# A linear-attention and mixture-of-experts kernel: state increment in column halves, loads behind K, an exponential in place, and spaced-out negations

## The chip, the cores and the metric

The kernel runs on one core of a Trainium2 chip. The metric is the device time of one execution in microseconds (us); of several executions the median is taken. Everything is float32 in memory; TensorE works on float32 (two passes, and so two load and two multiply records, per multiply) and on float32 rounded to its own short form, named fp32r (one pass).

## The reference

Two stages follow each other: a gated linear attention with a complex decay, and a mixture of four experts with two matrices each.

```python
mag = np.sqrt(a_re * a_re + a_im * a_im)
scale = np.minimum(mag, 0.999) / (mag + 1e-06)
a_re_n, a_im_n = (a_re * scale, a_im * scale)
for t in range(S):                      # S = 768, B = 4, H = 8, D = 48
    new_re = ar * S_re - ai * S_im
    new_im = ar * S_im + ai * S_re
    kv = np.einsum('bhd,bhe->bhde', k[:, :, t], v[:, :, t])
    S_re, S_im = (new_re + kv, new_im)
    y[:, :, t] = np.einsum('bhd,bhde->bhe', q[:, :, t], S_re)
# x: y as (3072, 384); E = 4 experts, F = 1024
p = domain_probs / (domain_probs.sum(-1, keepdims=True) + 1e-09)
for e in range(E):
    h = np.maximum(x @ w1[e], 0.0)
    out += p[:, e:e + 1] * (h @ w2[e])
```

## The kernel before, in words

The 3072 rows are cut into 12 groups (g) of 256 rows, each of two chunks (c) of 128. In the first part of the program, up to some 597 us, TensorE computes the first two experts of group g-1 (`moe1`: `w1_step` writes `ph`, `w2_step` writes `po`) while the other engines prepare the attention of group g. In the second part (`fast_path` from the pool `fin` on) it computes the other two experts with a scheme of fewer products, whose order is written out by hand in the table `UNIT`.

Attention of one group: `norm` scales the decay A to a magnitude below 1 (squares, a logarithm, an exponential, one correction step, on ScalarE and VectorE). `prefix` forms the running products of A along the rows on VectorE. `finish` makes Q = q times A and K = k over A. Both are put into a layout by head: for groups 0 and 1 with TensorE, later by a trip through device memory (`trip`: Q to `q_d` to `Qst`, K to `k_d` to `Kst`), whose transfers the queue of SyncE (SP) issues. Then come, for each chunk, functions of `chunk`: `turned` turns K with TensorE (`ktp`) and ScalarE copies it to `KT` (112 columns a head: the real part in columns 0 to 47, zeros, the imaginary part from column 64 on); `scores` multiplies `Kst` and `Qst` (`sc`); `values` makes the output (`yp`, by pairs of heads whose results stand in partitions 0 to 63 and from 64 on), and `increment` adds K times v to the state (`dp`, 8 multiplies a chunk, 20 chunks: the last chunk of each of the 4 sequences needs none). `turn_x` and `store_y` pass y on.

What stands in which order: the first part is ordered by a scheduler that lists the instructions of each engine by its own estimate of times; `stream`, `advance` and `between` say in what order work is handed to it, and `behind` ties one instruction behind another. Loads of the next group's q, k and a (`load_qk`, `load_a`) are tied behind the last transfer of the group before (`last["q"]`), that is the return of K in most groups. In the second part `UNIT` is read row by row by `unit`: M is a multiply, C a copy, D a sum, H and L the hidden layer, F a piece of the second matrix, and ("B", n) does up to n pieces from the list `side`: preparing the next x (`prep_x`), and for the second matrix of the next half expert the negated copy (`rest` in `second_w`: ScalarE writes `slo` from `shi`, and then GpSimd's queue adds the weights to it by a transfer). A piece "gap" in `side` makes it wait for so many B rows.

In `norm` the two buffers `s` and `u` hold four values: m2 and L in `s`, y0 and v in `u`. The exponential (L396) reads L and writes y0, so it is the first to write `u`, whose space was that of Q of a group before, which the trip to `q_d` reads.

Of the kernel before, what the change touches and what calls it, by code (L numbers as in the profile page):

```python
# [8 lines left out]
F32 = mybir.dt.float32  # L9
F32R = mybir.dt.float32r  # L10
AF = mybir.ActivationFunctionType
# [4 lines left out]
B, H, S, D = 4, 8, 768, 48  # L16
HD = H * D
NT = B * S
E, F = 4, 1024
# [14 lines left out]
M = 112  # L34
IM = 64
# [21 lines left out]
NSEL = 2  # L57
# [64 lines left out]
def fast_path(ctx, tc, qkP, aP, vP, probsP, w, out, flag):  # L122
    nc = tc.nc
# [25 lines left out]
    for c in range(CG):  # L149
# [8 lines left out]

    late_d = {(e, h): dram.tile([P, 2, len(WORDER) * P], F32, name=f"late_d{e}_{h}")
              for e, h in ((E1, 0), (E1 + 1, 0), (E1 + 1, 1))}  # L160

    wts = {}
    whi = {}
# [127 lines left out]
    with ExitStack() as c1:  # L291
# [82 lines left out]
        last = {}  # L374

        def norm(g, A, parts=((0, SEG),), prev=(None, None)):
            s = tmp(f"s{g}")
            u = tmp(f"u{g}")
            for n, (lo, hi) in enumerate(parts):
                col = g if n == 0 else NG  # L380
                fs = slice(lo * MS, hi * MS)
                Af = A.rearrange("p c i m -> p c (i m)")[:, :, fs]
                m2, L, y0, v = s[:, 0, fs], s[:, 1, fs], u[:, 0, fs], u[:, 1, fs]
                ins = [nc.scalar.activation(m2, Af[:, 0], AF.Square)]
                sq = nc.scalar.activation(L, Af[:, 1], AF.Square)
                ins.append(nc.vector.tensor_tensor_reduce(m2, m2, L, scale=1.0, scalar=3e38,
                                                          op0=ALU.add, op1=ALU.min, accum_out=st_m2[:, col:col + 1]))
                for x, p in zip(ins + [sq], prev + prev[:1]):
                    if p is not None:
                        behind(x, p)  # L390
                if n > 0:
                    behind(ins[0], exp)
                    behind(sq, exp)
                yield 1.0
                ln = nc.scalar.activation(L, m2, AF.Ln, bias=m2b)
                exp = nc.scalar.activation(y0, L, AF.Exp, scale=-0.5, bias=lnb)  # L396
                if g == 1:
                    behind(ln, state["kt", 0, 1])
                    behind(exp, state["kst", 0, 1])
                if g == 0 and n == 0:  # L400
                    nc.vector.tensor_tensor(v, m2, y0, op=ALU.mult)
                    nc.vector.scalar_tensor_tensor(v, v, 4.0 / CAP ** 2, y0, op0=ALU.mult, op1=ALU.mult)
                else:
                    last["sq"] = nc.scalar.activation(v, y0, AF.Square, scale=2.0 / CAP)
                    nc.vector.tensor_tensor(v, m2, v, op=ALU.mult)
                last["lin"] = nc.scalar.activation(L, y0, AF.Identity, scale=2.0 * EPS / CAP, bias=neg1)
                yield 0.95
                nc.vector.scalar_tensor_tensor(y0, v, 3.0, y0, op0=ALU.subtract, op1=ALU.mult)
                yield 0.95
                nc.scalar.activation(v, v, AF.Square, bias=neg1, accum_out=st_w[:, col:col + 1])  # L410
                nc.vector.scalar_tensor_tensor(y0, y0, -1.0, L, op0=ALU.max, op1=ALU.mult)
                yield 0.95
                nc.vector.tensor_tensor(Af, Af, bc2(y0), op=ALU.mult)
                yield 1.75
# [132 lines left out]
        def chunk(g, c, K, y):  # L547
# [27 lines left out]
            def increment():  # L575
                if last:
                    return
                d_ps = ps_a.tile([M, H, D], F32, tag="pa", name=f"dp{g}_{c}")
                for h in range(H):
                    ins = nc.tensor.matmul(d_ps[:, h, :], KT[:, h, :], vc[:, h * D:(h + 1) * D], start=True, stop=True)  # L580
                    if g == 0 and c == 1:
                        behind(ins, wts["w1"])
                state["dp", g, c] = ins
                Gt = small.tile([M, H, D], F32, tag="G", name=f"G{g}_{c}")
                if first:
                    nc.scalar.activation(Gt, d_ps, AF.Copy, scale=-1.0)
                else:
                    nc.vector.tensor_tensor(Gt, state[g, c], d_ps, op=ALU.subtract)
                state[g, c + 1] = Gt
# [275 lines left out]

        def stream():
            for g in range(1, NG):
                qk = load_qk(g, last["q"])
                if g + 1 < NG:
                    A.append(load_a(g + 1, prev=last["q"]))  # L870
                for r in front(g, A[g], qk):
                    yield g, r
                if g + 1 < NG:
                    for r in norm(g + 1, A[g + 1]):
                        yield g, r
# [53 lines left out]
    with ExitStack() as c2:  # L929
# [289 lines left out]
        def unit(R, h, fill):  # L1219
            e = E1 + R // NB2  # L1220
            assert ("w", e, h) in ready
            W = quads[e, h]

            def at(x):
                return bank(x) if isinstance(x, int) else snap[f"C{h}" if x == "C" else x]

            k = 0
            for op in UNIT:
                if op[0] == "M":
                    _, r, b, start = op  # L1230
                    n = XOF[r]
                    assert ("x", R, n) in ready
                    prod(bank(b), W[r], X[n], start)
                    if h == 1 and last_use[n] == r:
                        freed.add(n)
                elif op[0] == "C":
                    act(at(op[1]), at(op[2]), scale=op[3] if len(op) > 3 else 1.0)
                elif op[0] == "D":
                    tt(at(op[1]), at(op[2]), at(op[4]), ALU.add if op[3] == "+" else ALU.subtract)
                elif op[0] in "HL":  # L1240
                    (hi_h if op[0] == "H" else lo_h)((R, op[2], 4 * h + op[1]), at(op[3]))
                elif op[0] == "F":
                    fill(k)
                    k += 1
                else:
                    bg(op[1])

        half = C2 * HD
# [11 lines left out]
        for R in range(NR2):  # L1260
            for h in range(2):
# [5 lines left out]
                if h == 0:  # L1267
                    side += todo_x[:1]
                    tail = []
                    if R == 0:  # L1270
                        side += todo_x[1:2] + [["gap", None, 4, None]] + late
                    elif R in (1, NB2):
                        casts, tail = fetch_w(E1 + 1, *((0, 10) if R == 1 else (1, 0)))
                        side += todo_x[1:2] + [["gap", None, 3, None]] + casts
                    else:
                        side += todo_x[1:2]
# [212 lines left out]
```

## Time and profile before

| | |
|---|---|
| median of 3 runs | 975.66 us (974.34 to 976.28) |
| the profiled execution's own time | 973.79 us |
| its span, first to last instruction | 972.0 us |
| matmuls (PE) busy, share of the span | 946.8 us, 97% |
| VectorE (DVE) busy | 739.2 us, 76% |
| ScalarE (ACT) busy | 478.2 us, 49% |
| granted TensorE clock, mean | 0.997 |

The profiled execution took 1.8 us more than its span, and 1.87 us less than the median of the runs. In the rows below, PE is TensorE's multiply, PEld its load of the stationary operand, and an entry like `[0.98 <-DVE pb L959]` says how long the engine was idle ahead of the row and what ended it. The ends of multiplies are modelled, so the argument goes by the starts of rows that follow each other. TensorE is busy nearly throughout from 50 us on; before that it waits for loads, norms and turned data.

### The profile page before, as it was taken

The numbers are of one execution on the slowest core, as the hardware profiler recorded it, in microseconds if no ns is written. First come the engines' busy times: TensorE is split into PE (matmuls) and PEld (weight loads), VectorE is DVE, ScalarE is ACT, GpSimd is POOL, SyncE is SP. The second block draws the span as 40 slices with busy tenths as digits, with TensorE's granted clock in tenths as the row PEclk, the third lists the DMA queues.
The fourth block names the chain that finished last, engine by engine and source line by source line (L and its number), as shares of the span: only waits on it lengthen the run. The fifth ranks groups of instructions, "written<-read, shape, count | busy, mean of one in ns | idle before, by whom it ended". The sixth has DMA issues, their size and how long they took to land.

```text
span 972.0 us, 17615 instructions
## 1 busy us (share of the span) xinstructions
PE 946.8 (97%) x6717; PEld 923.0 (95%) x6717; DVE 739.2 (76%) x1610; ACT 478.2 (49%) x952; POOL 165.7 (17%) x206
## 2 busy tenths in 40 slices
PE   5899999999999999999999999999999999999997
PEld 3799999999999999999999999899999999999997
DVE  7889989898998889878897375767584857576642
ACT  7756436355363735446254355545453545445430
POOL 6020000000000000000000025433433352322000
PEclk9999999999999999999999999999999999999999
DMA  9586276684856647484669399232514443131112
GB/s 299 188 157 161 66 188 145 158 167 141 181 135 152 169 124 178 133 220 112 167 159 346 146 275 271 61 100 66 144 44 134 161 113 106 50 98 50 50 50 77
DMA packets 112238, 139.56 MB, mean 144 GB/s; under 512 B 8016, under 2 KB 95872, under 8 KB 112144
## 3 DMA queue, kind: packets, MB, share of 16 engines
q1 hardware_dynamic: 100656, 111.42, 40.0%
q0 software_dynamic: 11488, 26.93, 11.8%
q8 instruction: 55, 0.90, 0.4%
q14 instruction: 39, 0.32, 0.1%
HBM read 89.82 MB, written 48.49 MB: 142 GB/s over the span
## 4 chain that ended last, share of the span: by engine, by line
PE 86%; DMA 4%; ACT 3%; DVE 3%; issue 1%; SPq 0%; DVEq 0%; ACTq 0%
PE pob L953 20%; PE ph L235 18%; PE po L256 17%; PE pb L953 17%; PE sc L595 4%; PE dp L580 2%; PE yp L617 2%; PE yp L612 2%; DMA Kst<-k_d 1%; PE ktp L562 1%; PE xp L647 1%; DMA k_d<-K 1%; DMA y_d<-y 1%; DMA xa<-y_d 1%; PE qp L452 0%
## 5 line engine op out<-in xcount | busy, mean ns | idle before, releaser
L953 PE MATMUL pob<-shi,hid 128*128 128x384 f32 x528 | 148.7, 335 | 0.5 <-DVE hid L962 0.5
L256 PE MATMUL po<-whi,hh 128*128 128x384 f32 x384 | 129.9, 339 | 0.9 <-ACT acc L725 0.9
L256 PE MATMUL po<-wlo,hh 128*128 128x384 f32 x384 | 128.9, 336 | 0.0
L245 ACT ACTIVATE hh<-ph 128x512 fp32r<-128x512 f32 x96 | 57.0, 594 | 114.9 <-PE ph L235 114.1
L965 POOL TENSOR_TENSOR Z<-Z 128x384 f32<-128x384 f32 x84 | 90.7, 1115 | 109.3 <-DVE xl L959 46.4
L235 PE MATMUL ph<-xha,whi 128*128 128x256 f32 x576 | 103.8, 287 | 1.2 <-ACT xha L222 1.2
L235 PE MATMUL ph<-xha,wlo 128*128 128x256 f32 x576 | 101.3, 283 | 0.0
L235 PE MATMUL ph<-xla,whi 128*128 128x256 f32 x576 | 100.7, 284 | 0.0
L953 PE MATMUL pb<-xh,shi 128*128 128x384 f32 x291 | 97.3, 336 | 1.0 <-DVE pb L959 1.0
L953 PEld LDWEIGHTS pob<-shi,hid 128*128 128x128 f32 x528 | 96.5, 188 | 1.2 <-DVE hid L962 1.1
L953 PE MATMUL pb<-xl,shi 128*128 128x384 f32 x288 | 96.4, 335 | 0.0
L953 PE MATMUL pb<-xh,slo 128*128 128x384 f32 x288 | 96.3, 335 | 0.0
L246 DVE SCALAR_TENSOR_TENSOR hl<-ph,hh 128x512 fp32r<-128x512 f32 x96 | 66.0, 687 | 34.8 <-ACT hh L245 34.1
L235 PEld LDWEIGHTS ph<-xha,whi 128*128 128x128 f32 x576 | 85.7, 190 | 2.9 <-ACT xha L222 1.7
L953 PE MATMUL pob<-slo,hid 128*128 128x384 f32 x264 | 88.3, 335 | 0.0
L256 PE MATMUL po<-whi,hl 128*128 128x384 f32 x384 | 84.9, 338 | 0.0
L235 PEld LDWEIGHTS ph<-xha,wlo 128*128 128x128 f32 x576 | 82.9, 191 | 0.0
L235 PEld LDWEIGHTS ph<-xla,whi 128*128 128x128 f32 x576 | 82.6, 191 | 0.2 <-issue 0.2
L956 ACT ACTIVATE SN<-pb 128x384 f32<-128x384 f32 x96 | 47.3, 492 | 67.1 <-PE pb L953 59.7
L959 DVE TENSOR_TENSOR xl<-Z,xh 128x384 fp32r<-128x384 f32 x104 | 59.9, 607 | 21.6 <-ACT xh L956 13.8
L256 PEld LDWEIGHTS po<-whi,hh 128*128 128x128 f32 x384 | 72.5, 189 | 1.5 <-ACT acc L725 1.3
L956 ACT ACTIVATE hid<-pb 128x384 fp32r<-128x384 f32 x76 | 37.2, 490 | 72.2 <-PE pb L953 71.8
(227 smaller groups left out, 2090.6 us busy)
## 6 DMA issues: line engine op xcount, KB each, us to landing
qk<-qkP SPq DMA_DIRECT2D x24, 384.0 KB, 7.2
acc_d<-acc POOLq DMA_DIRECT2D x24, 384.0 KB, 5.2
ACC<-acc_d SPq DMA_DIRECT2D x48, 192.0 KB, 3.0
A<-aP SPq DMA_DIRECT2D x22, 384.0 KB, 8.2
Z<-y_d SPq DMA_DIRECT2D x16, 384.0 KB, 4.5
q_d<-Q SPq DMA_DIRECT2D x12, 387.0 KB, 4.1
Qst<-q_d SPq DMA_DIRECT2D x12, 387.0 KB, 5.5
v<-vP SPq DMA_DIRECT2D x24, 192.0 KB, 2.4
```

Source lines behind the costliest of these rows:

```text
L235: ins = nc.tensor.matmul(ph[:, u, :], wt[:, j * P:(j + 1) * P], xt[:, j, :], start=(n == 0), stop=(n == 3 * NJ - 1))
L245: wts["hh"] = nc.scalar.activation(hh, ph, AF.Relu)
L246: nc.vector.scalar_tensor_tensor(hl, ph, 0.0, hh, op0=ALU.max, op1=ALU.subtract)
L256: ins = nc.tensor.matmul(po[t], part[0][:, u, t * P:(t + 1) * P], wts[i][n][:, HD:], start=(i % FE == 0 and part[0] is hh and n == 0), sto ...
L580: ins = nc.tensor.matmul(d_ps[:, h, :], KT[:, h, :], vc[:, h * D:(h + 1) * D], start=True, stop=True)
L595: ins = nc.tensor.matmul(s_ps[:, h, :], Kc[:, hf * 4 + h, :], Qc[:, hf * 4 + h, :], start=True, stop=True)
L612: ins = nc.tensor.matmul(yo, st[:, o:o + n], Qc[:, o // D, :], start=True, stop=False)
L617: ins = nc.tensor.matmul(yo, vc[:, o:o + n], sc[h // 4][:, h % 4, :], start=first, stop=True)
L953: return tc.keep_in_program_order(nc.tensor.matmul(*args, **kw))
L956: return pin(nc.scalar.activation(dst, src, fn, scale=scale))
L959: pin(nc.vector.tensor_tensor(dst, x, y, op=op))
L965: nc.gpsimd.tensor_tensor(dst, x, y, op=op)
```

## The change

There are four edits.

1. **State increment by column halves.** Each of the 8 multiplies of `increment` becomes two: columns 0 to 63 of `KT` into partitions 0 to 63, and columns 64 to 111 into partitions 64 to 111. v, the moving operand (48 columns), is streamed for each.
2. **Next loads behind K.** From group 3 on, a transfer of one element from `Kst` to device memory (`here_d`) is issued on SP ahead of the loads of q, k and a. It reads `Kst`, so SP's queue stands until K has landed.
3. **Exponential in place.** In `norm` m2 and y0 share `s`, v and L share `u`; the exponential reads and writes the same place, and the first to write `u` is the square behind it (L404 before).
4. **Late negations one by one.** In the first unit of the second part the four negations of a half expert stand apart by gaps of one, and one ("B", 2) row is read four rows later in the unit (R, h) = (0, 1), and only there.

```diff
-    ("F",), ("D", 1, 0, "+", "B"), ("H", 1, 1, "F"), ("B", 2),
+    ("F",), ("D", 1, 0, "+", "B"), ("H", 1, 1, "F"), ("B", 2, 0),
     ("M", 15, 4, False), ("H", 3, 0, 4),
-    ("M", 18, 2, False), ("L", 1, 1, "F"), ("L", 3, 0, 4), ("D", 3, 2, "+", "E"),
+    ("M", 18, 2, False), ("L", 1, 1, "F"), ("L", 3, 0, 4), ("D", 3, 2, "+", "E"), ("B", 2, 1),
...
+    here_d = dram.tile([1, 1], F32, name="here_d")
...
-                m2, L, y0, v = s[:, 0, fs], s[:, 1, fs], u[:, 0, fs], u[:, 1, fs]
+                m2, y0, v, L = s[:, 0, fs], s[:, 1, fs], u[:, 0, fs], u[:, 1, fs]
                 ins = [nc.scalar.activation(m2, Af[:, 0], AF.Square)]
-                sq = nc.scalar.activation(L, Af[:, 1], AF.Square)
-                ins.append(nc.vector.tensor_tensor_reduce(m2, m2, L, scale=1.0, scalar=3e38,
+                sq = nc.scalar.activation(y0, Af[:, 1], AF.Square)
+                ins.append(nc.vector.tensor_tensor_reduce(m2, m2, y0, scale=1.0, scalar=3e38,
...
-                ln = nc.scalar.activation(L, m2, AF.Ln, bias=m2b)
-                exp = nc.scalar.activation(y0, L, AF.Exp, scale=-0.5, bias=lnb)
+                ln = nc.scalar.activation(y0, m2, AF.Ln, bias=m2b)
+                exp = nc.scalar.activation(y0, y0, AF.Exp, scale=-0.5, bias=lnb)
...
-                    ins = nc.tensor.matmul(d_ps[:, h, :], KT[:, h, :], vc[:, h * D:(h + 1) * D], start=True, stop=True)
-                    if g == 0 and c == 1:
-                        behind(ins, wts["w1"])
+                    for o, n in ((0, IM), (IM, D)):
+                        ins = nc.tensor.matmul(d_ps[o:o + n, h, :], KT[:, h, o:o + n], vc[:, h * D:(h + 1) * D],
+                                               start=True, stop=True)
+                        if g == 0 and c == 1:
+                            behind(ins, wts["w1"])
...
+                if g > NSEL:
+                    here = nc.sync.dma_start(here_d, Kst[0:1, 0, 0, 0:1])
+                    behind(here, last["q"])
+                    last["q"] = here
                 qk = load_qk(g, last["q"])
...
-                else:
+                elif len(op) == 2 or (op[2] == 1) == ((R, h) == (0, 1)):
                     bg(op[1])
...
-                        side += todo_x[1:2] + [["gap", None, 4, None]] + late
+                        side += todo_x[1:2] + [["gap", None, 3, None]]
+                        for x in late:
+                            side += [x, ["gap", None, 1, None]]
```

The scheduler orders the first part anew. What its list of TensorE makes of the increment is shown for group 7, chunk 0. Before, the 8 multiplies of `dp` stand together between `ph` and `sc`:

```order
L235 MATMUL ph_2_4184<-xha_3956,whi_548 128x256 x3
L580 MATMUL dp_0_4126<-v_0_4112,KT 112x48 x8
L595 MATMUL sc_0_0_4137<-Qst,Kst 128x128 x4
L595 MATMUL sc_0_1_4144<-Qst,Kst 128x128 x4
L235 MATMUL ph_2_4184<-xha_3956,wlo_549 128x256 x3
```

Now, at the same increment (its first rows of sixteen halves):

```order
L237 MATMUL ph_3_4378<-xha_4058,wlo_569 128x256
L583 MATMUL dp_0_4229<-v_0_4215,KT 64x48
L237 MATMUL ph_3_4378<-xha_4058,wlo_569 128x256
L583 MATMUL dp_0_4229<-v_0_4215,KT 48x48
L583 MATMUL dp_0_4229<-v_0_4215,KT 64x48
L583 MATMUL dp_0_4229<-v_0_4215,KT 48x48
```

The first half stands alone, a multiply of the expert follows, and then come the other fifteen halves. Over the whole list the 20 increments stand in 35 unbroken stretches: 6 in one, 13 in two, 1 in three; in 13 of them a stretch has an odd number of halves. The pairs of `yp`, which are column halves already before, stand in 29 stretches before and in 32 now.

On ScalarE, at the norm that is done beside the last pieces of group 4 (near 244 us in the profile), the exponential stood ahead of the copies `acc` of the experts' result from `po`, before:

```order
L490 ACTIVATE u_2427<-u_2427,a2e 128x24x16
L395 ACTIVATE s_2918<-s_2918,m2b 128x768
L396 ACTIVATE u_2919<-s_2918,lnb 128x768
L404 ACTIVATE u_2919<-u_2919 128x768
L406 ACTIVATE s_2918<-u_2919,neg_83 128x768
L245 ACTIVATE hh_0_3003<-ph_0_2984 128x512
L725 ACTIVATE acc_1_3019<-po_4_0_2732,pr 128x384
L725 ACTIVATE acc_1_3019<-po_4_1_2733,pr 128x384
```

and now:

```order
L247 ACTIVATE hh_0_3080<-ph_0_3061 128x512
L397 ACTIVATE s_2994<-s_2994,m2b 128x768
L729 ACTIVATE acc_1_3096<-po_4_0_2800,pr 128x384
L729 ACTIVATE acc_1_3096<-po_4_1_2801,pr 128x384
L398 ACTIVATE s_2994<-s_2994,lnb 128x768
L247 ACTIVATE hh_1_3137<-ph_1_3118 128x512
L406 ACTIVATE u_2995<-s_2994 128x768
L408 ACTIVATE u_2995<-s_2994,neg_83 128x768
```

The exponential no longer writes `u`; the copies and one `hh` have moved ahead of it and of the square that writes `u` first.

At the start of the second part (604 to 609 us in the profile), ScalarE's negations `slo` from `shi` stood in pairs, before:

```order
L956 ACTIVATE SN<-pb_7096 128x384
L956 ACTIVATE slo_6998<-shi_6993 128x384 x2
L956 ACTIVATE hid_7198<-pb_7139 128x384
L956 ACTIVATE shi_7206<-SN 128x384
L956 ACTIVATE slo_6999<-shi_6994 128x384 x2
L956 ACTIVATE slo_7215<-pb_7142 128x384
```

and now:

```order
L964 ACTIVATE slo_7168<-shi_7163 128x384
L964 ACTIVATE SN<-pb_7266 128x384
L964 ACTIVATE slo_7168<-shi_7163 128x384
L964 ACTIVATE hid_7368<-pb_7309 128x384
L964 ACTIVATE shi_7376<-SN 128x384
L964 ACTIVATE slo_7169<-shi_7164 128x384
L964 ACTIVATE slo_7383<-pb_7312 128x384
L964 ACTIVATE slo_7169<-shi_7164 128x384
```

One negation of each pair has moved: the first ahead of the copy `SN`, the last behind the `slo` that is made from `pb` (a hidden value kept in that buffer).

## The prediction

> **What bounds the kernel now.** I read the table of stretches first, then the chain that ended last, then the list of what TensorE waited for, then single stretches of the timeline. The first row below is the stretch from 50 to 600 us (its length, then busy time of PE, PEld, DVE, ACT, POOL); the second is the page's chain by engine.
>
> ```profile
> 50.00:600.00 550.00, 546.88 (x4388) 533.14 (x4389) 462.16 (x1057) 268.08 (x504) 39.52 (x50) 1.00 0.66 172
> PE 86%; DMA 4%; ACT 3%; DVE 3%; issue 1%; SPq 0%; DVEq 0%; ACTq 0%
> ```
>
> TensorE is busy in 546.88 of 550 us at the full granted clock (1.00). So in the first part a microsecond less on TensorE is a microsecond less at the end, unless a wait takes its place, and VectorE, busy in 462 of 550, has room for that. What is left is some 3 us of waits (550 - 546.88). An edit can therefore gain in two ways: less time of TensorE's own, or one of the few waits gone. Differences under 0.2% of the time (1.95 us) can't be told from no change here.
>
> **The increment in halves.** First the price before. Columns: start, duration of the merged rows, engine, line.
>
> ```profile
> 501.11 0.40 PE L235 MATMUL ph<-xha,whi 128*128 128x256 f32 x2
> 501.34 1.68 PE L580 MATMUL dp<-v,KT 128*112 128x48 f32 x16
> 502.84 0.36 PE L235 MATMUL ph<-xha,whi 128*128 128x256 f32 x1
> 503.05 0.52 PE L235 MATMUL ph<-xha,wlo 128*128 128x256 f32 x3
> 403.48 0.33 PE L256 MATMUL po<-wlo,hh 128*128 128x384 f32 x1
> 403.65 0.86 PE L256 MATMUL po<-whi,hl 128*128 128x384 f32 x4
> 404.44 0.43 PE L612 MATMUL yp<-Qst,G 112*48 112x128 f32 x4
> 404.80 0.62 PE L235 MATMUL ph<-xha,whi 128*128 128x256 f32 x3
> 405.26 0.52 PE L235 MATMUL ph<-xha,wlo 128*128 128x256 f32 x3
> 405.61 0.28 PE L235 MATMUL ph<-xla,whi 128*128 128x256 f32 x1
> 448.36 0.39 PE L617 MATMUL yp<-scs,v 128*48 128x128 f32 x4
> ...
> 449.68 0.39 PE L617 MATMUL yp<-scs,v 128*48 128x128 f32 x4
> ```
>
> Three `ph` records cost 0.36 us (405.61 - 405.26 = 0.35, starts rounded; 0.119 each), a `po` 0.17 (403.65 - 403.48). From 501.11 to 503.05 stand three `ph` (0.36) and one increment, so an increment of 16 records costs 1.94 - 0.36 = 1.58 us, 0.099 a record, with nothing lost at its ends. Twenty of them: 31.6 us.
>
> The halves don't occur before, but `yp` is worked in the same way: two heads in two column halves. From 448.36 to 449.68 stand 24 records in 1.32 us, so two records, one in each half, take 0.110 us together. The ends cost something: from 403.65 to 405.26 (1.61 us) stand four `po` (0.69), three `ph` (0.36) and four `yp` (two slots of 0.110); 0.34 us is left over. I read that as the price of going into column halves and out again, to be paid for each unbroken stretch.
>
> Now the price of a slot (a record in each half) of the increment. What its record waits for now is the load of 112 columns: v has 48 columns to stream against `yp`'s 128 in 0.110 us, which would be 0.041. These are the loads (mean ns after the bar) and the first loads of the `yp` stretch at 404.44:
>
> ```profile
> L580 PEld LDWEIGHTS dp<-v,KT 128*112 128x112 f32 x320 | 34.0, 178 | 0.0
> L617 PEld LDWEIGHTS yp<-scs,v 128*64 128x64 f32 x48 | 5.7, 136 | 0.2
> L617 PEld LDWEIGHTS yp<-scs,v 128*48 128x48 f32 x336 | 21.8, 123 | 1.8 <-DVE A L424 0.5 <-issue 0.4 <-DVE scs L600 0.3
> 404.44 0.17 PEld L612 LDWEIGHTS yp<-Qst,G 112*48 112x48 f32 x4 [0.25 <-issue]
> ```
>
> A load of 64 columns is 42 ns shorter than one of 112, so 0.099 - 0.042 = 0.057 us; by columns 0.099 x 64/112 = 0.057 as well. The last row says that the two halves load at the same time: four loads of 48 columns, 0.123 us each with their latency, are over in 0.17 us; one behind another, 0.042 apart (by columns again), they would need 0.25. So a slot is set by its wider load: 0.057 us. That is the low end; the high end is both loads in a row, 0.099, the row of now. I take 0.057, since the `yp` rows are the nearest.
>
> The count is in the new order: 20 increments of 16 slots, and 13 of them have two slots more, because a half stands alone and its partner too: 346 slots x 0.057 = 19.7 us. 35 stretches x 0.34 = 11.9 us. Sum 31.6 us, against 31.6 before: **0.0**. What is won by parallel loads is lost in going in and out, since the order breaks 14 of 20 increments into two or three. Three more stretches of `yp` (32 against 29): **+1.0 us**. All of it lies on TensorE, the engine that sets the end, with no cover.
>
> **Loads behind K.** SP's rows of group 7, the median times to landing of the page's list (issues, KB, us), TensorE at the two places where it waited for K, and the use of the held load:
>
> ```profile
> 337.26 1.41 SPq L528 DMA_DIRECT2D Kst<-k_d  x2
> 338.71 0.95 SPq L342 DMA_DIRECT2D qk<-qkP  x2
> 339.70 0.95 SPq L333 DMA_DIRECT2D A<-aP  x2
> 352.16 0.33 SPq L553 DMA_DIRECT2D v<-vP  x1
> qk<-qkP SPq DMA_DIRECT2D x24, 384.0 KB, 7.2
> Qst<-q_d SPq DMA_DIRECT2D x12, 387.0 KB, 5.5
> Kst<-k_d SPq DMA_DIRECT2D x12, 384.0 KB, 6.7
> 343.10 1.68 PE L580 MATMUL dp<-v,KT 128*112 128x48 f32 x16
> 345.40 0.80 PE L595 MATMUL sc<-Qst,Kst 112*128 112x128 f32 x5 [0.62 <-issue]
> 300.35 1.68 PE L580 MATMUL dp<-v,KT 128*112 128x48 f32 x16
> 302.19 1.05 PE L595 MATMUL sc<-Qst,Kst 112*128 112x128 f32 x7 [0.16 <-DMA Kst<-k_d]
> 365.61 1.82 DVE L492 TENSOR_TENSOR Q<-A,qk 128x768 f32<-128x768 f32 x2
> ```
>
> The loads of q, k and a are issued within 2.4 us of K's return and share the transfers with it; K takes 6.7 us where the equally large return of Q takes 5.5. Held, they start when the second half of K, issued near 338.3, has landed: some 5.5 us later, near 344, and at 7.2 us each land near 352; `Q` uses q at 365.61, so 13 us of slack cover the hold. Behind the waiting SP instruction stand the loads of q, k and a and then v, which was issued only at 352.16, so it waits for nothing new. The transfer of one element takes a place in the queue and nobody waits for it: no cost. The gain: `sc` comes after an increment of 1.58 us, at 344.68 and 301.93 instead of 345.40 and 302.19: 0.72 + 0.26 = **-1.0 us**. At least 1.2 us earlier (6.7 - 5.5) covers both. What is late next there is nothing that the rows show.
>
> **Exponential in place.** ScalarE and TensorE near 245 us:
>
> ```profile
> 245.12 0.94 ACT L396 ACTIVATE u<-s,lnb 128x768 f32<-128x768 f32 x1 [0.75 <-DMA q_d<-Q]
> 247.53 0.52 PE L235 MATMUL ph<-xla,whi 128*128 128x256 f32 x3
> 248.77 0.45 PE L256 MATMUL po<-whi,hh 128*128 128x384 f32 x1 [0.72 <-ACT acc L725]
> ```
>
> The exponential waited for the trip of Q, and behind it the copies `acc` that free `po` came late. `po` should have started at 247.53 + 0.36 = 247.89: a wait of 0.88. Now the copies stand ahead of it: **-0.9 us**. Elsewhere the wait only passes from the exponential to the square behind it, 0.94 us later, and TensorE didn't wait: nothing. The number of instructions stays.
>
> **Negations.** TensorE and ScalarE at the start of the second part:
>
> ```profile
> 608.11 0.34 PE L953 MATMUL pb<-xl,shi 128*128 128x384 f32 x1
> 609.42 0.44 PE L953 MATMUL pb<-xh,shi 128*128 128x384 f32 x1 [0.98 <-DVE pb L959]
> 607.01 0.92 ACT L956 ACTIVATE slo<-shi 128x384 fp32r<-128x384 f32 x2
> 607.84 0.47 ACT L956 ACTIVATE slo<-pb 128x384 fp32r<-128x384 f32 x1
> 628.50 0.51 ACT L956 ACTIVATE xh<-Z 128x384 fp32r<-128x384 f32 x1
> 629.72 0.34 PE L953 MATMUL pob<-slo,hid 128*128 128x384 f32 x1
> 630.60 0.62 PE L953 MATMUL pob<-shi,hid 128*128 128x384 f32 x2 [0.54 <-DVE hid L962]
> ```
>
> At 609.42 TensorE waits for a sum in `pb` that VectorE can form only after `slo` from `pb` has been copied, and that copy stands behind two negations (0.92). One now follows it: 0.46 us less of a wait of 1.14 (609.42 - 608.11 - 0.17): **-0.5**. At 630.60 it waits 0.71 us for `hid`; the ("B", 2) row that is read four rows later takes a copy `xh` (0.51, at 628.50) and the difference `xl` that follows it out from ahead of `hid`, some 0.9 us in all: the whole wait, **-0.7**. A negation that comes later delays its transfer, which the next half unit uses microseconds later: nothing.
>
> **The sum.** 0.0 + 1.0 - 1.0 - 0.9 - 0.5 - 0.7 = -2.1 us, from 973.79 to 971.7 for the profiled execution. That execution was 1.87 us faster than the median, so I put the difference on the median: 975.66 - 2.1 = **973.6 us**. Bounds of the unknown terms: a slot of 0.062 would cost 1.7 us more; the stretch's price, if 0.30, 1.5 us less; the waits gone, if they return in part, 0 to 1.9 us more.
>
> **Rivals.**
> *The halves load and multiply one after another.* If no weights load while a multiply is in flight, a slot is 0.057 + 0.041 = 0.098 us: 346 x 0.041 = 14.2 us more, 987.8 us: slower. It decides from a slot of 0.063 on (0.057 + 2.1/346), where the gains are eaten. Against it speaks `yp`: load 0.042 and stream some 0.11 would make 0.15, and the row shows 0.110 for both. For it: no row shows a slot as short as 0.057. The Trainium skill, "TensorE: Matmul & The Clock Gate" (Part 3, what overlaps and what doesn't), says that weight loads overlap with multiplies in flight only where the row groups differ, and here they are the same; the rows of `yp` disagree with it.
> *Going in and out costs the increment nothing.* If its short streams hide the change, 35 x 0.34 = 11.9 us fall away: 961.7 us. For it: the 0.34 was read only from `yp`, whose streams are longer; against: each `yp` stretch, short or long, paid it. The Trainium skill, "TensorEngine Tiling (Array Packing)" (Theoretical Speedup), gives up to twice the rate for 64 columns; by that alone the increment would fall to half, an estimate of 15.8 us less. The rows of `yp` confirm the rate inside a stretch and not the ends.
> *The waits come back.* The first part is scheduled anew by estimates, and the places where TensorE waited were few and accidental; if the 1.9 us of the second and third edit turn up again at other places, it ends at 975.5, and with one more wait of that size (1.0) at 976.5: no change.
>
> **Chances.** My forecast 0.55, one after another 0.12, nothing for the ends 0.13, waits come back 0.20. Around my forecast I allow 2 us to each side. Of its 0.55 I put 0.36 over 0.2% faster and 0.18 within: more than half, since the median run has 1.87 us more than the profiled one, and what varies from run to run is above all the transfers on which the second and third edit no longer wait. So faster is 0.36 + 0.13 + 0.01 = 0.50, same 0.18 + 0.15 = 0.33, slower 0.01 + 0.04 + 0.12 = 0.17. The range leaves out the slow rival (0.12) and the larger part of the fast one (0.08): from 967.5 (half of the ends' price gone) to 978.0 (waits back and a slot of 0.061). Where the likely cases alone hold, it is 971.6 to 976.5.
>
> **What would show it.** In the changed profile two records of `dp` should take 0.057 us together, a stretch's ends 0.34, and all `dp` about as long as before; `sc` at K's return and `po` behind `acc` should show no wait; the wait at 609 should be near 0.7 and that at 630 gone. A slot near 0.10, a stretch without the 0.34, or new waits of over 2 us in the first part would prove me wrong.

## The result and the profile after

The changed kernel takes 982.18 us (median of 7 runs, 981.11 to 989.45) where the kernel before takes 975.73 (974.34 to 976.28) beside it: a ratio of 1.0089, interval 1.0061 to 1.0117. It is slower, by 6.5 us between the medians, where 2 us faster had been forecast. The profiled execution was the slowest of the seven (989.45 us, span 987.6, mean clock 0.988), 7.3 us above the median; so the waits shown below are larger than those of a median execution, and explain its own 15.7 us over the profiled execution before, not the 6.5.

The same views as before. The table of stretches from 50 to 600 us, and the chain by engine:

```profile
50.00:600.00 550.00, 536.71 (x4590) 514.38 (x4590) 454.92 (x1040) 260.95 (x488) 27.67 (x39) 0.99 0.63 163
PE 75%; DMA 12%; DVE 6%; ACT 3%; issue 1%; SPq 0%; DVEq 0%; ACTq 0%
```

TensorE is idle for 13.3 us of this stretch (3.1 before), and the transfers' share of the chain has gone from 4% to 12%. What TensorE waited for, and below it what VectorE waited for at its masking of the scores (us in total, times, longest):

```profile
PE sc L599 <- DMA Kst<-k_d: 11.5, 7, 3.4
...
PE sc L599 <- ACT Kst L574: 0.6, 1, 0.6
...
DVE scs L604 <- PE sc L599: 21.9, 22, 4.4
```

The kernel before has these groups too:

```profile
PE sc L595 <- issue: 0.6, 1, 0.6
...
PE sc L595 <- DMA Kst<-k_d: 0.4, 2, 0.2
PE sc L595 <- DMA Qst<-q_d: 0.3, 1, 0.3
...
DVE scs L600 <- PE sc L595: 7.3, 12, 1.7
```

TensorE's waits at the scores have grown from 1.3 to 12.1 us. The longest stand in groups 5, 6 and 11. Two of them on TensorE's timeline (start, duration of the merged rows, and the wait ahead in brackets):

```profile
259.07 0.32 PE L583 MATMUL dp<-v,KT 128*64 128x48 f32 x2
261.82 0.77 PE L599 MATMUL sc<-Qst,Kst 112*128 112x128 f32 x2 [2.44 <-DMA Kst<-k_d]
312.49 2.89 PE L599 MATMUL sc<-Qst,Kst 112*128 112x128 f32 x13 [3.36 <-DMA Kst<-k_d]
```

SP's timeline ahead of the second, K's trip of group 6 and the loads behind it:

```profile
301.17 0.38 SPq L523 DMA_DIRECT2D k_d<-K  x1
304.69 3.37 SPq L530 DMA_DIRECT2D Kst<-k_d  x2
310.03 0.23 SPq L873 DMA_DIRECT2D here_d<-Kst  x1
310.30 0.83 SPq L344 DMA_DIRECT2D qk<-qkP  x2
```

The hold does a part of what was meant: q is issued at 310.30, after K's first half, and not within 2.4 us of K's issue. But `here_d` reads partition 0 of `Kst`, which only the first of K's two transfers writes, so the queue doesn't stand until the whole of K has landed: q goes out 2 us before the second half lands, at whose landing the scores begin (312.49). The scores stand where K hasn't landed, and a wait costs more than its length. Rows of the table of stretches behind the waits that end at 261.82, 312.49 and 541.34 (the last number but two is the granted clock), and one behind a shorter wait (1.30 us, to 359.61):

```profile
262.00:266.00 4.00, 4.00 (x40) 3.69 (x41) 1.01 (x4) 0.00 (x0) 0.00 (x0) 0.50 1.17 224
266.00:270.00 4.00, 4.00 (x23) 3.57 (x22) 3.04 (x8) 0.00 (x0) 0.00 (x0) 0.70 0.76 290
312.50:316.50 4.00, 4.00 (x20) 4.00 (x21) 1.60 (x3) 0.23 (x1) 0.00 (x0) 0.57 0.84 326
...
359.60:363.60 4.00, 3.99 (x34) 3.69 (x35) 2.75 (x7) 0.00 (x0) 0.00 (x0) 1.00 0.91 338
541.40:545.40 4.00, 4.00 (x21) 4.00 (x22) 3.36 (x7) 0.63 (x1) 0.00 (x0) 0.57 1.07 308
```

By the clock alone, four us at 0.50 cost 2.0; in the same way these stretches lose 2.0 + 1.2 + 1.7 + 1.7 = 6.6 us. With the 10.8 us of added waits that is 17.4, and the first multiply of the second part (`pb`) starts 17.1 us later than before (611.05 against 593.98). That accounts for the first part. The second part answers to the forecast (last below).

The price of the increment. An unbroken one on TensorE's timeline in the changed kernel:

```profile
53.96 0.52 PE L237 MATMUL ph<-xla,whi 128*128 128x256 f32 x3
54.41 1.13 PE L583 MATMUL dp<-v,KT 128*64 128x48 f32 x32
55.47 0.62 PE L237 MATMUL ph<-xla,whi 128*128 128x256 f32 x3
55.93 0.52 PE L237 MATMUL ph<-xha,whi 128*128 128x256 f32 x3
```

From 53.96 to 55.93 stand six `ph` (6 x 0.119) and the increment: 1.97 - 0.72 = 1.25 us, where 16 x 0.057 + 0.34 = 1.25 had been forecast. The multiply itself is as it should be.

### The profile page after: what moved, and what is told of

It reads as the page before. It is cut to its first block, busy times and chain, and to the rows that moved or that the text cites. A ratio compares the mean times of both kernels' runs of the same rounds, so it can differ in the third digit from the quotient of the medians.

```text
span 987.6 us, 18277 instructions
## 1 busy us (share of the span) xinstructions
PE 952.5 (96%) x7037; PEld 920.5 (93%) x7037; DVE 739.5 (75%) x1610; ACT 479.6 (49%) x952; POOL 165.9 (17%) x206
## 3 DMA queue, kind: packets, MB, share of 16 engines
q0 software_dynamic: 11488, 26.93, 11.7%
## 4 chain that ended last, share of the span: by engine, by line
PE 75%; DMA 12%; DVE 6%; ACT 3%; issue 1%; SPq 0%; DVEq 0%; ACTq 0%
PE pob L961 20%; PE pb L961 17%; PE ph L237 13%; PE po L258 13%; PE sc L599 5%; DMA Kst<-k_d 4%; DMA k_d<-K 4%; PE yp L621 2%; PE yp L616 2%; DMA q_d<-Q 2%; PE dp L583 1%; DVE K L513 1%; DMA y_d<-y 1%; PE ktp L564 1%; DVE Q L494 1%
## 5 line engine op out<-in xcount | busy, mean ns | idle before, releaser
L967 DVE TENSOR_TENSOR xl<-Z,xh 128x384 fp32r<-128x384 f32 x104 | 59.8, 606 | 21.1 <-ACT xh L964 10.9
L258 PEld LDWEIGHTS po<-wlo,hh 128*128 128x128 f32 x384 | 72.8, 190 | 0.0
```

The costliest lines, as they stand in the source:

```text
L258: ins = nc.tensor.matmul(po[t], part[0][:, u, t * P:(t + 1) * P], wts[i][n][:, HD:], start=(i % FE == 0 and part[0] is hh and n == 0), sto ...
L967: pin(nc.vector.tensor_tensor(dst, x, y, op=op))
```

## The experiments

Each kernel was timed against the kernel before on the same chip, with 4 to 12 executions of its own.

### The four edits one at a time

Each kernel is the one before with one edit of the change; a line or two of each stand here, the rest is as in the diff of the change.

```diff
# halves alone
+                    for o, n in ((0, IM), (IM, D)):
# hold alone
+                if g > NSEL:
+                    here = nc.sync.dma_start(here_d, Kst[0:1, 0, 0, 0:1])
# exponential alone
+                exp = nc.scalar.activation(y0, y0, AF.Exp, scale=-0.5, bias=lnb)
# negations alone
+                        for x in late:
+                            side += [x, ["gap", None, 1, None]]
```

> The kernel before with the increment in column halves alone. Theory 1 (the hold costs: behind it the scheduler thinks K returns sooner and puts the scores earlier, and TensorE waits for K): here no hold, so only the counted cost of the halves, 0 to +2 us, 975.5 to 978, and waits of TensorE for K of under 2 us in all. Theory 2 (the halves cost: shorter in the scheduler's eyes, they pull the scores ahead of K): +4 to +8 us, 980 to 984, with waits for K of 5 us or more. Both expect a slot of two half records near 0.057 us and 0.34 us for a stretch's ends, so an increment in one piece near 1.25 us.

> The kernel before with the next loads held behind K alone. Theory 1 (the hold costs by the order): +4 to +8 us, 980 to 984, with waits of TensorE for K of 5 us or more although K itself returns in 5 us or less instead of 6.7. Theory 2 (the halves cost): -1 to 0 us, 974.5 to 976, K's return shorter and waits for K under 1 us.

> The kernel before with the exponential in place alone. Both theories: -1 to +1 us (974.5 to 977), the one wait of TensorE for the copies of the experts' result (0.88 us near 249 us) gone or moved. A third theory (the new order of ScalarE around the norm delays K on VectorE): +3 us or more, with waits for K.

> The kernel before with the late negations one by one alone. All theories: the first part of the program is the same as before, the waits in the second part at 609 and 630 us fall from 1.14 to about 0.7 and from 0.71 to 0: -0.8 to -1.5 us, 974 to 975.

| | us | ratio to before |
|---|---|---|
| halves alone | 985.3 | 1.0106 (1.0091 to 1.0121) |
| hold alone | 974.44 | 1.0002 (0.9992 to 1.0011) |
| exponential alone | 974.02 | 0.9999 (0.9990 to 1.0008) |
| negations alone | 973.08 | 0.9988 (0.9979 to 0.9997) |

The halves carry the whole loss (somewhat over the 980 to 984 us of theory 2), and the hold none of it: the theory that the hold's tie turns the order against K has fallen. The four ratios add up to 1.0095, within the interval of the whole change. What TensorE waited for at the scores in the halves alone, and VectorE's wait for the scores:

```profile
PE sc L597 <- DMA Kst<-k_d: 7.3, 3, 4.6
PE sc L597 <- issue: 4.6, 3, 2.4
...
PE sc L597 <- DMA Qst<-q_d: 1.2, 1, 1.2
...
PE sc L597 <- DMA lw<-w: 0.8, 1, 0.8
...
DVE scs L602 <- PE sc L597: 27.0, 20, 5.6
```

13.9 us, against 1.3 before. The longest of them, on TensorE's timeline:

```profile
303.12 1.13 PE L581 MATMUL dp<-v,KT 128*64 128x48 f32 x32
308.81 3.78 PE L597 MATMUL sc<-Qst,Kst 112*128 112x128 f32 x16 [4.55 <-DMA Kst<-k_d]
```

VectorE's timeline of the same kernel:

```profile
305.08 0.25 DVE L424 TENSOR_TENSOR A<-pf 128x96 f32<-128x96 f32 x1
310.92 0.69 DVE L602 TENSOR_TENSOR scs<-sc,maskp 128x512 f32<-128x512 f32 x1 [5.59 <-PE sc L597]
```

TensorE waits for K, VectorE for the scores behind it, and everything behind that on VectorE, the next group's K among it, comes later as well.

### Without the halves

The change without its first edit.

```diff
-                    for o, n in ((0, IM), (IM, D)):
-                        ins = nc.tensor.matmul(d_ps[o:o + n, h, :], KT[:, h, o:o + n], vc[:, h * D:(h + 1) * D],
+                    ins = nc.tensor.matmul(d_ps[:, h, :], KT[:, h, :], vc[:, h * D:(h + 1) * D],
```

> The change without its first edit: whole increments, the other three edits in. New theory, order: the cost of the change is where the scheduler, once the increments are halves, puts K's product on VectorE against the scores on TensorE; with whole increments the lists of TensorE and VectorE are those of before up to the exponential and the negations, so TensorE should wait for K at no place by more than 0.3 us, and the gains of the three edits alone add up: -1.4 (negations) -0.5 (exponential) 0.0 (hold) from 974.5, 972.6 us, ratio 0.998. Rival, the other edits disturb too: with all three in, waits appear that none showed alone, and it ends at 975 or above.

973.44 us against 974.70; ratio 0.9988 (0.9977 to 0.9999). TensorE waits for K at one place, 0.4 us. It lies 0.8 us above the 972.6 expected, but under the rival's 975. Like the negations alone, at the same ratio, it beats both kernels, by a margin hardly above the measurement's.

### What the lists say

If the multiply costs what it did, why does K come late? The lists of the instructions show it without any time. VectorE's list before, from the state's increment of group 9 to the product K of group 10 and on:

```
888 L588 TENSOR_TENSOR G9_1_5378<-G9_0_5194,dp9_1_5369 112x384
889 L511 TENSOR_TENSOR K10_5384<-A10_4498,u210_4970 128x8x6x16 x2
890 L405 TENSOR_TENSOR u11_5439<-s11_5438,u11_5439 128x768
891 L635 TENSOR_TENSOR P2_156<-G9_1_5378,TB_158 48x384
892 L636 TENSOR_TENSOR P2_156<-G9_1_5378,TB_158 48x384
893 L246 SCALAR_TENSOR_TENSOR hl8_5_5469<-ph8_5_5449,hh8_5_5468 128x512
```

and with the halves:

```
889 L640 TENSOR_TENSOR G9_1_5514<-G9_1_5514,P2_156 112x384
890 L405 TENSOR_TENSOR u11_5575<-s11_5574,u11_5575 128x768
891 L509 TENSOR_TENSOR u210_5090<-qk10_5083,u210_5090 128x768
892 L246 SCALAR_TENSOR_TENSOR hl8_6_5653<-ph8_6_5633,hh8_6_5652 128x512
893 L408 SCALAR_TENSOR_TENSOR u11_5575<-u11_5575 128x768
894 L224 TENSOR_TENSOR xla9_5669<-xa9_5485,xha9_5668 128x768
895 L511 TENSOR_TENSOR K10_5520<-A10_4610,u210_5090 128x8x6x16 x2
```

Before, K stands ahead of the rotation of the state (P2), of the norm of group 11 (u11) and of the experts' rests hl8_5 and hl8_6; with the halves they stand ahead of K. The scores of group 10 haven't moved against the experts: in both lists they follow as many `ph` and `po` (worth 310.1 us at 0.119 and 0.173). So the scheduler leaves less between K's product and the scores. The table counts VectorE's instructions from the end of K's product to the first masking of the scores, for groups 6 to 11, beside what TensorE waited at the scores in all in the profiled execution, that execution's time, and the median:

| kernel | VectorE instructions, K to scores, groups 6 to 11 | TensorE's waits at `sc`, us | profiled us | median us |
|---|---|---|---|---|
| before | 20 17 23 39 40 51 | 1.3 | 973.8 | 974.7 |
| changed | 18 21 17 26 24 43 | 12.1 | 989.5 | 982.2 |
| halves alone | 18 21 17 26 24 43 | 13.9 | 989.8 | 985.3 |
| halves in groups 6 to 11 | 19 16 23 24 24 43 | 7.1 | 982.6 | 985.9 |
| halves, scores handed over later | 23 18 22 29 32 46 | 7.9 | 991.3 | 989.9 |
| halves, 20 multiplies for 16 | 20 17 23 39 40 52 | 2.9 | 979.8 | 977.5 |
| halves, 24 for 16 | 23 21 25 37 44 60 | 2.6 | 983.0 | 983.5 |
| halves, 32 for 16 | 45 48 62 65 84 45 | 0.2 | 997.4 | 997.4 |

The counts say where an instruction stands and not how long it takes: group 7 has more of them with the halves (21 for 17) and waits all the same. So here are times from the traces for groups 6 to 11, in us. "Room" runs from the end of K's product to where TensorE would have begun the scores (their start less the wait ahead of it), "trip" from the same end to the landing of K's second half:

| kernel | room | trip |
|---|---|---|
| before | 11.1 9.3 9.6 18.9 19.1 17.9 | 11.3 9.8 8.9 14.3 13.8 17.7 |
| halves alone | 7.7 9.8 7.9 11.2 10.5 14.3 | 12.3 11.8 10.2 10.1 12.1 15.0 |
| halves in groups 6 to 11 | 10.7 7.7 10.4 9.1 11.9 17.4 | 11.5 11.7 8.6 9.7 12.6 14.7 |
| halves, 20 multiplies for 16 | 11.4 9.1 9.7 19.8 19.1 22.0 | 10.9 9.4 10.3 15.3 15.1 19.4 |

TensorE waits where the trip is longer than the room. With the halves alone the room shrinks in five of the six groups, by 3.4 us in group 6 and by some 8 in groups 9 and 10. But in groups 6 to 8 the trip also takes 1.0 to 1.9 us longer, and in group 7 the wait comes from that alone. With 20 multiplies for 16 the room is as before or wider, within 0.3 us, and the trips of groups 6 to 8 add up to 30.5 us, against 34.3 with the halves alone and 30.0 before. So the longer trips go with the order and not with the halves as such; with which transfers they share the queues wasn't tried apart.

### Halves in the last groups only, and scores handed over later

Two kernels tried the theory by moving the order by hand; a third did the latter with all four edits.

```diff
# halves in groups 6 to 11
+                    for o, n in ((0, IM), (IM, D)) if g >= 6 else ((0, M),):
# scores later
-FIRST = {1: 5, 2: 5, 3: 4, 4: 4, 5: 3, 6: 3}
+FIRST = {1: 5, 2: 5, 3: 4, 4: 4, 5: 3, 6: 4, 7: 3, 8: 3, 9: 3, 10: 3, 11: 3}
```

> Halves only in groups 6 to 11 (10 of the 20 increments), whole ones in groups 0 to 5. In the lists the scores of groups 6 to 8 then stand as far behind K's product as before, those of groups 9 and 10 nearly as near as with all halves. Theory order: no wait for K of over 0.5 us in groups 6 to 8, 0.5 to 2 us each in groups 9 to 11, 976 to 978.5 us. Rival, halves: half of the halves, half of the cost, 979.9 us, spread over the groups.

985.86 us; ratio 1.0120 (1.0100 to 1.0139). Half of the halves, and the whole cost: the rival's 979.9 is out, and so is the theory's 976 to 978.5. The waits in groups 9 and 10 came about as expected (0.7 us each; in group 11 there was none), but group 6 has one of 0.9 and group 7 one of 4.0 us (to 349.00), though the counts had hardly moved. The trace shows where a part of the 4.0 us comes from. VectorE's timeline around K's product of group 7, before, and with halves in groups 6 to 11:

```profile
333.65 1.82 DVE L511 TENSOR_TENSOR K<-A,u 128x768 f32<-128x768 f32 x2
335.39 0.95 DVE L408 SCALAR_TENSOR_TENSOR u<-u 128x768 f32<-128x768 f32 x1
```

```profile
332.23 0.96 DVE L405 TENSOR_TENSOR u<-s,u 128x768 f32<-128x768 f32 x1 [0.99 <-ACT u L404]
334.57 0.95 DVE L408 SCALAR_TENSOR_TENSOR u<-u 128x768 f32<-128x768 f32 x1
335.44 1.82 DVE L511 TENSOR_TENSOR K<-A,u 128x768 f32<-128x768 f32 x2
```

A piece of the next group's norm (L408) stands ahead of K now, and another (L405) has VectorE waiting 0.99 us for ScalarE; so K's product ends 1.8 us later (337.26 against 335.47), and 5.2 us of experts' multiplies are left between it and the scores, against 6.9. In addition K's trip took 11.65 us from the end of its product to its landing, against 9.84 before; why, isn't shown.

> Halves alone, with the attention of groups 6 to 11 handed to the scheduler one expert step later (FIRST 3 in place of 2; 4 for group 6). In the lists the scores then stand 1.5 to 5.6 us of experts' multiplies later, K's product where it stood. Theory order: of the waits for K in the halves alone (4.56, 2.04, 2.53, 1.1, 1.62 and 0.83 us in groups 6 to 11) some 2.4 and 0.5 are left in groups 6 and 7 and nothing in the others; 985.3 falls by 9 to 11 us to 974.5 to 977. Rival, halves: the cost belongs to the column halves themselves (going in and out, slower experts' multiplies beside them), so with 35 stretches as before the time stays at 983 to 987 whatever the scores wait for.

989.87 us; ratio 1.0148 (1.0131 to 1.0166): slower still, and far from the theory's 974.5 to 977. As a repair this failed. The waits at the scores did fall, from 13.9 to 7.9 us, but the step later brought another, of 4.7 us, for the copies `acc` that free `po`.

Moving the attention by hand moves other things too, so this run can't tell the theories apart.

> All four edits, and the attention of groups 6 to 11 handed over one expert step later as in the run of halves alone with later scores. Theory order: the changed kernel's waits for K (2.44, 3.37, 1.30, 1.20, 0.68 and 2.08 us in groups 5 to 11) go except in group 5 and in part in group 6, and the negations give their 1.4: 973 to 976 us, ratio 0.998 to 1.002. Rival, halves: it stays at 980 or above.

982.18 us; ratio 1.0080 (1.0064 to 1.0095), as long as the changed kernel itself. Of its 12.1 us of waits at the scores 5.1 are left, and again a wait for `acc` (4.0 us) takes the place of those that went. Here too the expected 973 to 976 was missed; the time is where the rival had it (980 or above), though with waits, and so this run doesn't part the two either.

### Useless halves added

To give the scheduler back its old view without touching what is handed over when, some heads are multiplied twice; the second result overwrites the first with the same values, so nothing but useless work is added.

```diff
-                    for o, n in ((0, IM), (IM, D)):
+                    for o, n in ((0, IM), (IM, D)) * (2 if h < 2 else 1):
```

> Halves alone, with useless work added: the halves of heads 0 and 1 of every increment are issued twice (20 multiplies for 16). In the lists this puts K's product back to where it stood before against the scores (39, 40 and 52 VectorE instructions between them in groups 9 to 11; 39, 40 and 51 before; 26, 24 and 43 with the plain halves). Theory lists: the halves cost as much on the chip as whole multiplies, and the 10.8 us come from the scheduler's reckoning a half too cheaply and so setting the scores too soon after K; then more work makes it faster: no wait for K over 1 us, and 40 slots of 0.057 more (2.3 us): 976 to 978 us. Rival, halves: the cost is in the column halves themselves; 985.3 + 2.3 = 987.6 us.

977.52 us; ratio 1.0027 (1.0016 to 1.0037). A quarter more multiplies, and 7.8 us less than the halves alone. TensorE's waits at the scores, and VectorE's for them:

```profile
PE sc L597 <- DMA Kst<-k_d: 1.5, 2, 0.8
...
PE sc L597 <- issue: 1.2, 3, 0.6
...
PE sc L597 <- ACT Kst L572: 0.2, 1, 0.2
...
DVE scs L602 <- PE sc L597: 10.8, 16, 1.6
```

This is the decisive run: the column halves are all there, the increments still in 32 stretches, and three quarters of the loss are gone; what is left (2.6 us over before) is less than the useless work costs (4.7, below). That the time fell into the expected 976 to 978 is partly luck: the useless work was put at 2.3 us and costs 4.7, and the halves in this order turned out some 2 us cheaper than whole multiplies. The rival is out by 10 us with the one price and by 12 with the other.

The next two repeat heads 0 to 3 (`h < 4`) and all eight (`h < 8`).

> The same with the halves of heads 0 to 3 issued twice (24 multiplies for 16); 37, 44 and 60 instructions between K and the scores in groups 9 to 11. Theory lists: no wait for K over 1 us, 80 slots of 0.057 more (4.6 us): 978.5 to 980.5 us. Rival, halves: 985.3 + 4.6 = 989.9 us.

983.47 us; ratio 1.0095 (1.0078 to 1.0113); 3 us above the expectation.

> The same with all halves issued twice (32 multiplies for 16); 65, 84 and 45 instructions between K and the scores in groups 9 to 11. Theory lists: no wait for K at all, 160 slots of 0.057 more (9.1 us) and two stretches more (0.7): 983.5 to 985.5 us, less than or equal to the plain halves with half of their work. Rival, halves: 985.3 + 9.8 = 995 us.

997.42 us; ratio 1.0228 (1.0208 to 1.0248); 12 us above it, and as recorded nearer to the rival's 995. All three expectations had counted the slots wrong: a repeated head is two halves of two passes, and so two slots, not one. The price of a slot comes from an unbroken increment with 32 slots, on TensorE's timeline of the kernel that repeats all heads:

```profile
54.38 0.52 PE L235 MATMUL ph<-xla,whi 128*128 128x256 f32 x3
54.83 2.06 PE L581 MATMUL dp<-v,KT 128*64 128x48 f32 x64
56.83 0.63 PE L235 MATMUL ph<-xla,whi 128*128 128x256 f32 x3
57.29 0.52 PE L235 MATMUL ph<-xha,whi 128*128 128x256 f32 x3
```

2.91 - 0.72 = 2.19 us; less 1.25 for 16 slots, and over 16: 0.059 us each. With that 4, 8 and 16 slots more in each of 20 increments cost 4.7, 9.4 and 18.9 us. Taken off, the three kernels stand at 972.8, 974.1 and 978.5 us, against 974.95 before. The first two leave the halves themselves at a gain of 1 to 2 us, with their remaining waits in. The third has other waits (5.6 us for `xha`, 1.2 before): in its trace TensorE stands idle 3.8 us longer than before from 50 us to the first `pb`, and 3.4 us at half the clock behind a wait of 2.46 us cost 1.7. Together that is 5.5 us, more than the 3.5 by which it stands above before. With the right count of slots the rival would have been at 990.0, 994.7 and 1004.2 us, 6.8 to 12.5 us above the three.

> All four edits, and the halves of heads 0 and 1 of every increment issued twice: the changed kernel with some useless work. In the lists K's product stands against the scores as before (39, 40 and 52 VectorE instructions between them in groups 9 to 11; 26, 24 and 43 in the changed kernel). A repeated head is two slots, two heads four (the expectations of the three runs before counted half of that); 4 x 20 slots of 0.059 are 4.7 us. Theory lists: the halves alone with this work took 977.5; the negations (-1.4) and the exponential (-0.5) come off: 975.6 us (974.5 to 976.8), ratio 1.0005, and no wait for K of over 1 us. Rival, halves: the changed kernel's 982.2 plus 4.7, 986.9 us.

975.18 us against 974.96; ratio 1.0005 (0.9995 to 1.0014), as the theory of the lists had it (975.6), 11.7 us away from the rival. TensorE's longest wait for K is 0.7 us. The changed kernel with 80 useless slots is 7 us faster than without them.

## Why the prediction was wrong

**Increment in halves: the price was right, the place was missing.** A slot was put at 0.057 us and measures 0.059; the ends of a stretch at 0.34, and measure 1.25 - 16 x 0.059 = 0.31. At these prices the increments of the changed kernel come to 346 x 0.059 + 35 x 0.31 = 31.3 us against the 31.6 forecast, but no run measures that sum, nor the +1.0 for `yp`, apart from the waits. The gain of 1 to 2 us in the kernels with useless slots doesn't contradict them, since those have another order: the one with heads 0 and 1 repeated stands in 32 stretches and not 35, 9 and not 13 of its increments are broken at an odd half, and `yp` stands in 28 stretches. By the same prices its halves come to 338 x 0.059 + 32 x 0.31 = 29.9 us, and `yp` to 0.3 less than before, some 2 us under the 31.6. The rivals "one after another" and "ends cost nothing" are both out. What failed is the step behind them: "All of it lies on TensorE, the engine that sets the end, with no cover." That took the rest of the order as given, and so the sum has no term for new waits; the bounds allow for waits that return, at most 1.9 us. In the profiled execution they were 10.8 us and 6.6 more at a lower clock. I had read in the new lists how the increment is broken up on TensorE, but not what becomes of K on VectorE, against which the scores are set.

**The rival "the waits come back" was the right one, mis-sized.** It was put at 0.9 to 1.9 us back and at no change (975.5 to 976.5), from the waits that the profile of before showed. They were short because that order happened to leave K enough time: in its groups 6 to 8 the trip of K took 11.3, 9.8 and 8.9 us from product to landing, and the scores came 11.3, 9.9 and 9.6 us after the product. That is 0.7 us of slack at most. The new order left less room, and in groups 6 to 8 of the halves alone K's trip was longer as well. So the waits came back not as the old ones at other places, as the rival had it, but as new ones at K. "New waits of over 2 us in the first part would prove me wrong" was the sentence that came true.

**Loads behind K: -1.0 forecast, 0.0 measured** (0.9992 to 1.0011). Alone it takes the waits for K away (in its trace the scores wait 0.3 us, for a copy). In that trace TensorE is busy 548.18 us from 50 to 600, 1.3 more than before; but this was the fastest of 11 executions (972.43 us), and the median hasn't moved. Of the reason given, that K returns sooner once the loads are held, the trace shows little: the list puts K at 6.9 us to landing, where it was 6.7 (5.5 in the changed kernel). And since the hold ends with K's first half, the loads still go out ahead of K's landing: in group 6 q is issued at 297.14, and K's second half lands at 300.64. "Held, they start when the second half of K ... has landed" was wrong. Why the median gains nothing isn't settled by these runs.

**Exponential in place: -0.9 forecast, -0.5 measured, no difference within the interval.** The wait it was meant to remove has gone down from 0.88 to 0.19 us. TensorE's timeline in the changed kernel:

```profile
248.32 0.52 PE L237 MATMUL ph<-xla,whi 128*128 128x256 f32 x3
248.87 0.45 PE L258 MATMUL po<-whi,hh 128*128 128x384 f32 x1
```

The copies `acc` (from 248.26) stand ahead of the exponential (249.19), and `po` starts 0.55 us after the three `ph` do (0.36 of it theirs).

**Negations: -1.2 forecast, -1.4 measured** (0.9979 to 0.9997), by both steps. TensorE's timeline in the changed kernel, at the first of the two places:

```profile
625.16 0.34 PE L961 MATMUL pb<-xl,shi 128*128 128x384 f32 x1
625.90 0.44 PE L961 MATMUL pb<-xh,shi 128*128 128x384 f32 x1 [0.41 <-DVE pb L967]
```

625.90 - 625.16 - 0.17 = 0.57 us, where a wait of 1.14 had been and "near 0.7" was forecast; the wait for `hid` twenty microseconds later is gone.

**What stays open.** That the order is the cause is shown by the runs with useless work. Why the scheduler leaves less time is read from its lists alone: K moves closer to the scores with 16 halves, back to its place with 20 and far away with 32, as if it went by how long the increment is reckoned to be; the reckoning itself wasn't looked at. And why K's trip is 1 to 2 us longer in groups 6 to 8 of the halves alone, and in group 7 with halves in the last groups only, stays open: what it shared the queues with wasn't tried apart.

## What to carry to other kernels

Where a scheduler orders the work, an edit that costs nothing on its own engine can cost ten microseconds through the order: compare the new lists of two engines at every transfer that had no slack before, and not only on the engine that was edited. Count what stands between a producer and its consumer in both lists, look also at what has moved ahead of the producer, and set the time between them against the time the trip took in the trace. To tell an instruction's own price from that of the order, add useless copies of it until the old order returns, and take their price off.

## What the runs showed of the hardware

**The clock can fall after waits of 2 us already.** In the traces of all the kernels of this case together, TensorE stood still for over 2 us fourteen times from 50 us on. Ten of these waits were under 3.4 us: seven (2.03, 2.08, 2.44, 2.46, 2.64, 2.80 and 3.36 us) were followed by a granted clock of 0.50, three (2.13, 2.41 and 2.50 us) were not. The four longer ones (4.04 twice, 4.56 and 4.67 us) all were, and none of the waits of 0.9 to 1.6 us was. The clock stood at 0.50 for 3.4 us, in three cases for 6.8, and fell at the latest 1.7 us behind the wait; a stretch of the table that lies in it only in part shows a value between, as the 0.57 above. Two rows of the table of stretches of the halves alone, behind the 4.56 us and behind the 2.41:

```profile
308.80:312.00 3.20, 3.19 (x15) 3.19 (x16) 1.08 (x2) 0.00 (x0) 0.00 (x0) 0.50 0.84 326
```

```profile
401.00:405.00 4.00, 3.96 (x51) 3.82 (x51) 1.34 (x4) 0.00 (x0) 0.00 (x0) 1.00 1.07 312
```

The Trainium skill, "TensorE: Matmul & The Clock Gate" (Part 1, "What's actually happening"), says that the clock halves after an idle window of about 3.4 us, and that the windows run freely. Here seven of the ten waits between 2 and 3.4 us, shorter than that window, were followed by a lower clock; the half that the page gives is what the traces show. What decides between the seven and the three isn't shown.

**Going into column halves and out again takes 0.31 us** of TensorE's time around the increment, much as around the longer streams of `yp` (0.34). The Trainium skill, "TensorEngine Tiling (Array Packing)" (Key Properties), says that a change of the tiling mode drains TensorE; the 0.31 and 0.34 us agree with a loss at each change, and whether a drain is what takes them isn't shown.
